# Values of the last 64 queries: two heads on the two column halves of TensorE, and x's transposes sorted by DMA

## The chip, the cores and the metric

The kernel runs on one core of a Trainium2 chip. The metric is the device time of one execution in microseconds, as the median of several runs. Beside it there is one profiled execution, in which the hardware recorded when each instruction of each engine started and how long it took. The engines are named as in the profile: PE (TensorE's matmuls) and PEld (its weight loads), DVE (VectorE), ACT (ScalarE), POOL (GpSimd), SP (SyncE, which here only issues DMAs).

## The reference

Attention over 8 batches of 8 heads, 576 positions of 64 numbers each, causal by blocks of 64, and behind it a layer of two products, their maximum and an output product.

```python
def _attn_ref(q, k, v):                      # (8, 8, 576, 64) float32
    B, H, S, D = q.shape
    block = 64
    scores = 1.0 / np.sqrt(D) * np.matmul(q, k.transpose(0, 1, 3, 2))
    pos = np.arange(S)
    mask = pos[:, None] // block >= pos[None, :] // block
    scores = np.where(mask, scores, -1000000000.0)
    scores = scores - np.max(scores, axis=-1, keepdims=True)
    attn = np.exp(scores)
    attn = attn / (np.sum(attn, axis=-1, keepdims=True) + 1e-09)
    return np.matmul(attn, v)

def _moe_ref(x, w1, w2, w_out):              # x is (4608, 512): all heads of a position in a row
    return np.maximum(x @ w1, x @ w2) @ w_out
```

576 is four and a half times 128, so the last tile of queries, and the last chunk of keys, has 64 positions.

## The kernel before, in words

**Pairs and groups.** A pair `p` is two heads of one batch; there are 32. Two pairs make a group `g` (16 groups), and two groups a batch. The two heads of a pair lie on the two halves of the 128 partitions in `qT` and `kT` (64 numbers each). Scores are made transposed, keys on the partitions and queries along the row, so that ACT's exponential writes `aT`, which is at once the stationary operand of the product with the values. `vv` holds the values with a column of ones behind them, 65 columns, so that the 65th column of the product is the sum to divide by.

**Values (`av`, L636).** For a tile `t` of 128 queries, head `hh` of the pair and each of the `t + 1` chunks `c` of keys: load 128 columns of `aT` as weights, stream the 65 columns of `vv`, add into `ps_o`, whose 128 partitions are the queries. The tile `t = 4` has only 64 queries; it is computed with all 128 columns, of which the upper 64 are padding (`aT`'s columns from 1600 on are zeros). A pair's tiles come in two calls, `[0, 1]` (6 matmuls) and `[2, 3, 4]` (24, ten of them for `t = 4`). After each call DVE takes the reciprocals of the sums (L658) and multiplies (L659) into `xp`, a tile for a group, laid out as position, head of the pair, tile, pair of the group, number.

**x transposed.** The second layer needs `xT`, features on the partitions and positions along the row. Groups 4 to 14 get it by DMA: `x_dma` (L668) issues two transposes a group on SP's queue, one for each `s` (L670), each of five blocks of 128 positions. The last block's upper half is padding, and lands on the first 64 positions of the next batch, which are written later. Groups 0 to 3 and 15 go through PE: `x_out` (L676) transposes 64 x 128 blocks into `ps_xe` (even blocks of 64 positions) and `ps_xo` (odd ones), and two copies bring them to `xT` (L695, L696).

**The second layer.** The maximum of two products is computed as one product with the difference of the weights (`d_sb`, in `h_unit`, L244), a relu, and what remains folded into the output product (`product`, L390, with `ps_p`). These units are a list of work that `fill(n)` draws from, so many matmuls at a time, as soon as `done_tokens` says that their positions of `xT` are there. The order on every engine is written out by hand; nothing is reordered at run time.

**The loop over groups** (from group 3 on), for each of a group's two pairs: filling matmuls; `av_with`, which is `av` of tiles 0 and 1 of the pair two back, some filling, `av` of tiles 2 to 4; behind the second pair of a group `x_dma` of the group before, and behind the first the DMA transposes of the next group's `k` (L147), also on SP's queue; the transposes of `q` through PE (L525); the scores of two tiles (L544, and L562 for the corner, where padded keys `kz` are used); their exponentials (L568) and masks. The transposes and scores use 64 partitions of operands each: PE works there as two halves of rows. SP's queue holds, in order, the output's stores, the loads of `q`, `k`'s transposes and `x`'s.

Of the kernel before, what the change touches and what calls it, by code (L numbers as in the profile page):

```python
# [8 lines left out]
FP32 = mybir.dt.float32  # L9
BF16 = mybir.dt.bfloat16  # L10
# [4 lines left out]
def kernel(  # L15
# [10 lines left out]
    nc = tc.nc  # L26

    B, H, S, D = q.shape
    P = 128
    BLK = 64  # L30
# [23 lines left out]
    NCH = 5  # L54
# [5 lines left out]
    def a_col(p, c, t):  # L60
        if p >= HP:
            return CB[c] + t * P
        late = t * P >= QCUT
        return t * P + {
            0: 384 - QCUT if late else 0, 1: 704 - QCUT if late else 256 - P,
            2: 1024 - QCUT, 3: 1408 - 3 * P, 4: 1344 - 4 * P,
        }[c]
# [14 lines left out]
    small = ctx.enter_context(tc.tile_pool(name="small", bufs=4))  # L82
    xpool = ctx.enter_context(tc.tile_pool(name="xp", bufs=3))
# [6 lines left out]
    ps_m = ctx.enter_context(tc.tile_pool(name="ps_m", bufs=4, space=bass.MemoryType.PSUM))  # L90
# [10 lines left out]
    xT = ring.tile([P, NDM, NTOK + BLK], BF16, name="xT")  # L101
# [4 lines left out]
    ident = wpool.tile([P, P], BF16, name="ident")  # L106
# [69 lines left out]
    for j in range(d_ff // WB):  # L176
        row, n = (1, j) if j < 3 else (3, 0)
        t0 = 3 * S - 3 * BLK + n * NDM * WB
# [309 lines left out]
    todo = [[n, u, need, cost] for u, need, cost, n in units]  # L488
# [28 lines left out]
    xps = {}  # L517
# [114 lines left out]
    def region(*tiles):  # L632
        for out in tiles:
            out()

    def av(p, ts):  # L636
        b, hp = divmod(p, HP)
        vv = vv_r[b % NV]
        a = aT_r[p % NA]
        n = len(ts)  # L640
        h0 = hp // 2 * 4 + hp % 2
        if p % 2 == 0 and ts[0] == 0:
            xps[p // 2] = xpool.tile([P, 2, NCH, 2, D], BF16, name="xp")
        xp = xps[p // 2]
        po = ps_m.tile([P, n, 2, D + 1], FP32, name="ps_o", tag="m")
        n_mm = 2 * sum(t + 1 for t in ts)
        mm = 0
        for gi, t in enumerate(ts):
            for hh in range(2):
                for c in range(t + 1):  # L650
                    a0 = a_col(p, c, t)
                    nc.tensor.matmul(  # L652
                        po[:, gi, hh, :], a[:, hh, a0:a0 + P], vv[:, c, h0 + 2 * hh, :],
                        start=(mm == 0), stop=(mm == n_mm - 1),
                    )
                    mm += 1
        rec = small.tile([P, 3, 2, 1], FP32, name="rec")
        nc.vector.reciprocal(rec[:, :n, :, 0], po[:, :, :, D])  # L658
        nc.vector.tensor_mul(  # L659
            xp[:, :, ts[0]:ts[0] + n, p % 2].rearrange("q s t d -> q t s d"), po[:, :, :, :D],  # L660
            rec[:, :n].to_broadcast([P, n, 2, D]),
        )

    def x_by_dma(g):
        return BY_DMA <= g < NG - 1

    def x_dma(g):
        b, u = divmod(g, GPB)  # L668
        for s in range(2):
            nc.sync.dma_start_transpose(  # L670
                out=xT[:, 2 * u + s, b * S:b * S + NCH * P].rearrange(
                    "p (t w) -> p t w", w=P),
                in_=xps[g][:, s].rearrange("p t a d -> p (t a d)"),
            )

    def x_out(g, t0=0, t1=NCH, copies=(dve, dve)):  # L676
        b, u = divmod(g, GPB)
        if x_by_dma(g):
            if u == GPB - 1:
                done_tokens[0] = (b + 1) * S  # L680
            return
        xp = xps[g]
        n = t1 - t0
        n_odd = min(t1, NCH - 1) - t0
        pe = ps_m.tile([P, 2, n, BLK], BF16, name="ps_xe", tag="m")
        po = ps_m.tile([P, 2, n_odd, BLK], BF16, name="ps_xo", tag="m")
        for s in range(2):
            for t in range(t0, t1):
                src = xp[:, s, t].rearrange("p a d -> p (a d)")
                nc.tensor.transpose(pe[:, s, t - t0, :], src[:BLK], ident[:BLK, :BLK])  # L690
                if t < NCH - 1:
                    nc.tensor.transpose(po[:, s, t - t0, :], src[BLK:], ident[BLK:, BLK:])
        dst = xT[:, 2 * u:2 * u + 2, b * S + t0 * P:b * S + t1 * P].rearrange(
            "p s (t h w) -> p s t h w", h=2, w=BLK)
        copies[0](out=dst[:, :, :, 0], in_=pe[:])  # L695
        copies[1](out=dst[:, :, :n_odd, 1], in_=po[:])  # L696
        if u == GPB - 1:
            done_tokens[0] = min(b * S + t1 * P, (b + 1) * S)

# [7 lines left out]
    def fill_of(g):  # L707
        if g == NG - 1:
            return 45
        left = 5 - g if g < 5 else 2 - (g - 5) % 2  # L710
        return -(-max(0, ready() - KEEP) // left)
# [35 lines left out]
    def av_with(p, n):  # L747
        av(p, [0, 1])
        fill(n)
        av(p, [2, 3, 4])  # L750
# [31 lines left out]
    ck((0,), HIGH, dve)  # L782
    ck((1,), HIGH, dve)
    av(0, [0, 1])
    warm_up(2)
    burst_p(3)
# [5 lines left out]
    av(2, [0, 1])  # L792
    warm_up(2)
    x_out(0, 0, 2, (act, act))
    av(3, [0, 1])
    diff_w(0)
# [4 lines left out]
    load_w(2)  # L801
    burst_q2(1)
    x_out(1, 0, 2)
    warm_up(2)
    burst_q3(1)
# [22 lines left out]
    for c in range(NCH):  # L828
        load_v(1, c)
    x_out(0, 2, NCH)  # L830
    diff_w(1)
    fill(2)
# [15 lines left out]
    n = fill_of(GPB)  # L848
# [10 lines left out]
    for g in range(GPB + 1, NG):  # L859
        a, b = 2 * g, 2 * g + 1  # L860
        old = done_tokens[0]
        if x_due:
            x_out(x_due.pop())
        n, new = fill_of(g), done_tokens[0]
        region(tile_0(a), tile_1(a))
        lo, hi = max(3, n // 18), n * 2 // 9 - 2 * (g < 5)
        for p, tiles in ((a, lambda: (tile_2(a), tile_0(b))), (b, lambda: (tile_1(b), tile_2(b)))):
            done_tokens[0] = old if p == a and x_by_dma(g - 2) else new
            fill(hi)
            av_with(p - LAG, lo)  # L870
            done_tokens[0] = new
            if p % 2 and x_by_dma(g - 1):
                x_dma(g - 1)
            if p % 2 == 0:
                for nm in "qk":
                    if g + 1 < NG and by_dma(nm, g + 1):
                        transpose_blocks(nm, g + 1)
            copy_out = t_pair(p)
            outs = tiles()
            copy_out()  # L880
            region(*outs)
            if p % 2 and g + 1 < NG:
                pad_keys(p + 1)
                pad_keys(p + 2)
            pool_work(p)
        x_due.append(g - 1)
        fill(n - 2 * (lo + hi))
    for p in range(NPAIR - LAG, NPAIR):
        if x_due:
            x_out(x_due.pop())  # L890
        av_with(p, 5)
        if p % 2 and x_by_dma(p // 2):
            x_dma(p // 2)
        fill(9)
# [42 lines left out]
```

## Time and profile before

| | us |
|---|---|
| median of 3 runs | 247.27 (247.2 to 248.71) |
| the profiled execution, its own time | 247.61 |
| its span, from the first instruction to the last | 245.8 |
| L652, values: one matmul's record, 960 of them | 0.194 |
| L652, values: one weight load's record | 0.098 |
| L659, multiply of 384 elements, 32 of them | 0.558 |
| L659, multiply of 256 elements, 32 of them | 0.424 |
| L658, reciprocal, 64 of them | 0.184 |
| L670, one transpose's time on SP's queue, median | 1.272 |
| L147, one transpose of `k` there, median | 1.429 |
| L121 and L409, a plain DMA there, the least | 0.367 |

An engine's busy time is the union of its instructions' records. Matmuls are pipelined, so the record of a short one is much longer than the step from it to the next. In a row such as `152.62 0.43 ... x18` the first number is the start from the span's beginning, the second the length of the run of 18 with the tail of the last. The granted clock of PE was 0.997 of full speed over the execution.

### The profile page before, as it was taken

How to read it: one execution, taken by the hardware profiler on the slowest of the kernel's cores; microseconds unless marked ns; L12 is line 12 of the kernel's file. 1: busy time of each engine (PE TensorE's matmuls, PEld its weight loads, DVE VectorE, ACT ScalarE, POOL GpSimd, SP SyncE). 2: the span in 40 equal slices, each digit the busy share in tenths (PEclk: the TensorE clock that was granted, in tenths of full speed). 3: DMA queues.
4: the chain of work that ended last, by engine and by line, in shares of the span. 5: the costliest groups of instructions: out<-in, count | busy, mean ns of one | idle time of the engine just before them, and what ended most of it. 6: DMA issues, size and time to landing. Idle time of an engine off the chain costs nothing.

```text
span 245.8 us, 7595 instructions
## 1 busy us (share of the span) xinstructions
PE 234.4 (95%) x3093; PEld 167.3 (68%) x3109; DVE 185.4 (75%) x395; ACT 143.8 (58%) x200; POOL 129.6 (53%) x294
## 2 busy tenths in 40 slices
PE   7689899999999999999999999999999999999993
PEld 2347666688865886588558755875587578567782
DVE  4976989999677958795879587957785788526573
ACT  2888871677677748673867386748673730462200
POOL 1996952669959584948593859485621210010000
PEclk9999999999999999999999999999999999999998
DMA  6999999579999999999999999999994321301125
GB/s 233 318 206 306 231 278 195 172 137 188 153 196 180 168 163 222 184 201 183 244 227 130 208 164 272 122 223 193 134 138 97 100 39 45 131 0 43 47 86 172
DMA packets 108867, 41.33 MB, mean 168 GB/s; under 512 B 89248, under 2 KB 102688, under 8 KB 108832
## 3 DMA queue, kind: packets, MB, share of 16 engines
q0 software_dynamic: 65952, 11.87, 69.4%
q1 hardware_dynamic: 42464, 28.32, 51.7%
q10 hardware_dynamic: 416, 0.66, 0.8%
q8 instruction: 24, 0.39, 0.7%
q14 instruction: 11, 0.09, 0.1%
HBM read 34.60 MB, written 9.44 MB: 179 GB/s over the span
## 4 chain that ended last, share of the span: by engine, by line
PE 87%; DVE 7%; ACT 4%; issue 1%; ACTq 0%
PE ps_p L390 35%; PE ps_h L244 24%; PE ps_o L652 11%; PE ps_s L544 9%; PE ps_w L514 3%; ACT aT L568 3%; PE ps_qT L525 2%; DVE sums L358 2%; DVE sums L364 1%; DVE g L252 1%; DVE m_sb L277 1%; PE ps_s L562 1%; PE ps_xe L690 1%; PE ps_bT L261 1%; DVE qT L533 1%
## 5 line engine op out<-in xcount | busy, mean ns | idle before, releaser
L568 ACT ACTIVATE aT<-ps_s 128x1024 bf16<-128x1024 f32 (+2 forms) x100 | 95.7, 994 | 32.1 <-PE ps_s L544 24.0
L244 PE MATMUL ps_h<-xT,d_sb 128*128 128x512 bf16 (+3 forms) x307 | 68.0, 357 | 1.0 <-DVE d_sb L191 0.3
L573 POOL MEMSET aT<- 64x128 bf16 x124 | 21.8, 200 | 52.8 <-ACT aT L568 51.9
L244 PEld LDWEIGHTS <-d_sb 128*128 128x128 bf16 x320 | 29.7, 98 | 26.7 <-issue 2.2
L652 PEld LDWEIGHTS <-aT 128*128 128x128 bf16 x960 | 37.2, 98 | 6.9 <-issue 0.8
L652 PE MATMUL ps_o<-vv,aT 128*128 128x65 bf16 x960 | 39.8, 194 | 0.3 <-DVE xp L659 0.3
L250 ACT ACTIVATE g<-ps_h 128x512 bf16<-128x512 f32 (+1 forms) x40 | 23.3, 587 | 23.3 <-PE ps_h L244 22.3
L165 POOL DMA_DIRECT2D vv<-in_v_dram x40 | 33.9, 857 | 1.1 <-issue 0.9
L252 DVE TENSOR_SCALAR g<-ps_h 128x512 bf16<-128x512 f32 (+2 forms) x40 | 23.6, 594 | 13.1 <-PE ps_h L244 12.8
L659 DVE TENSOR_TENSOR xp<-ps_o,rec 128x256 bf16<-128x256 f32 (+1 forms) x64 | 31.4, 491 | 2.2
L544 PE MATMUL ps_s<-qT,kT 64*128 64x64 bf16 (+6 forms) x344 | 31.3, 280 | 1.8 <-ACT kT L533 0.7
L390 PE MATMUL ps_p<-sums,bT_sb 128*128 128x256 bf16 x216 | 32.8, 273 | 0.0
L390 PEld LDWEIGHTS <-bT_sb 128*128 128x128 bf16 x288 | 27.5, 98 | 4.5 <-issue 1.4
L138 POOL DMA_DIRECT2D kb<-in_k_dram x40 | 29.5, 765 | 0.0
L533 ACT COPY qT<-ps_qT 128x576 bf16<-128x576 bf16 (+1 forms) x17 | 10.3, 614 | 23.2 <-PE ps_qT L525 23.2
L390 PEld LDWEIGHTS <-g 128*128 128x128 bf16 x220 | 19.8, 98 | 4.8 <-issue 2.8
L390 PE MATMUL ps_p<-wo_sb,g 128*128 128x256 bf16 (+1 forms) x148 | 22.7, 270 | 0.0
L161 POOL CAST qn<-qraw 128x1152 bf16<-128x1152 f32 (+1 forms) x16 | 17.1, 1067 | 5.1 <-DMA qraw<-in_q_dram 5.1
L544 PEld LDWEIGHTS <-kT 64*128 64x128 bf16 x344 | 12.2, 94 | 10.5 <-issue 5.1
L658 DVE RECIPROCAL rec<-ps_o 128x4 f32<-128x4 f32 (+1 forms) x64 | 11.8, 184 | 6.8 <-PE ps_o L652 6.8
L236 POOL COPY g<-g 128x512 bf16<-128x512 bf16 x8 | 5.9, 733 | 20.6 <-ACT g L250 20.3
L364 DVE TENSOR_TENSOR bT_sb<-g 128x1024 bf16<-128x1024 bf16 x18 | 12.4, 688 | 5.4 <-ACT g L250 4.8
(90 smaller groups left out, 326.1 us busy)
## 6 DMA issues: line engine op xcount, KB each, us to landing
qraw<-in_q_dram SPq DMA_DIRECT2D x16, 576.0 KB, 6.0
out_dram<-y SPq DMA_DIRECT2D x35, 256.0 KB, 3.9
vv<-in_v_dram POOLq DMA_DIRECT2D x32, 128.0 KB, 7.3
kraw<-in_k_dram SPq DMA_DIRECT2D x5, 576.0 KB, 7.4
kb<-in_k_dram POOLq DMA_DIRECT2D x40, 72.0 KB, 6.8
w1raw<-in_moe_w_dram POOLq DMA_DIRECT2D x4, 512.0 KB, 8.8
xT<-in_moe_w_dram POOLq DMA_DIRECT2D x4, 256.0 KB, 9.2
wo_sb<-in_moe_w_out_dram POOLq DMA_DIRECT2D x2, 512.0 KB, 10.9
```

Source lines behind the costliest of these rows:

```text
L138: nc.gpsimd.dma_start(out=n[h * BLK:(h + 1) * BLK, :, s], in_=(q if nm == "q" else k)[b, 4 * u + 2 * s + h].rearrange("(j p) d -> p j d", ...
L161: copy(out=n[:, j0:j1], in_=t[:, j0:j1])
L165: nc.gpsimd.dma_start(out=vv_r[b % NV][P - rows:, c, :, :D], in_=v[b, :, c * P:c * P + rows, :].rearrange("h p d -> p h d"),)
L244: nc.tensor.matmul(pt[:, :w], d_sb[:, c, f * P:(f + 1) * P], xT[:, c, t0:t0 + w], start=(c == 0), stop=(c == NDM - 1),)
L250: nc.scalar.activation(out=g[:, f, m:m + w], in_=pt[:, :w], func=AF.Relu)
L252: nc.vector.tensor_scalar_max(g[:, f, m:m + w], pt[:, :w], 0.0)
L390: nc.tensor.matmul(pt[:, q0:q0 + w], lhs[c][:, s * P:(s + 1) * P], rhs[c][:, m:m + w], start=(c == 0 and q0 == 0), stop=(c == 5 and q0 + w ...
L544: nc.tensor.matmul(ps[:, hh, col:col + w], kT[r, k0:k0 + P], qT[r, q0:q0 + w], start=True, stop=True,)
L568: nc.scalar.activation(out=aT_r[p % NA][:, :, a0:a0 + w], in_=ps[:, :, :w], func=AF.Exp, scale=scale,)
L573: (eng or nc.gpsimd).memset(aT_r[p % NA][BLK:, :, a0:a0 + BLK], 0.0)
L652: nc.tensor.matmul(po[:, gi, hh, :], a[:, hh, a0:a0 + P], vv[:, c, h0 + 2 * hh, :], start=(mm == 0), stop=(mm == n_mm - 1),)
L659: nc.vector.tensor_mul(xp[:, :, ts[0]:ts[0] + n, p % 2].rearrange("q s t d -> q t s d"), po[:, :, :, :D], rec[:, :n].to_broadcast([P, n, 2 ...
```

## The change

The last tile's ten matmuls of a pair take 64 columns of `aT` instead of 128 as weights, alternately for the two heads. Head 0's output goes to partitions 0 to 63 of `ps_o`, head 1's to partitions 64 to 127 of the same columns, and the matmul's place in the array follows from that: 128 rows, and the lower or upper 64 columns. In the built program the 320 matmuls of this kind have a tile of 128 x 64 at column 0 or 64; the other 640 stay as they were. They come last in the call, chunk by chunk, head by head.

`ps_o` of a `[2, 3, 4]` call has five slots instead of six, and so have the reciprocal and the multiply. `xp` is laid out as nine blocks: tiles 0 and 1 of head 0, of head 1, tiles 2 and 3 of head 0, the shared last tile, tiles 2 and 3 of head 1; `x_blk` gives the place. Each call writes one stretch of it.

`x_dma` issues five transposes a group instead of two: tiles 0 and 1 of either head (two blocks each), tiles 2 to 4 of head 0 (three blocks), tiles 2 and 3 of head 1 (two), and from partitions 64 to 127 of the shared block head 1's last 64 positions. In the built program the first two of them wait for the multiply of the `[0, 1]` call. `x_out` transposes the shared block's lower half for both `s`, its upper half once more, and overwrites the wrong 64 columns with one further copy of 64 columns.

```diff
+    def x_blk(s, t):
+        return t + 2 * s if t < 2 else 6 if t == NCH - 1 else t + 2 + 3 * s
+
     def av(p, ts):
...
-            xps[p // 2] = xpool.tile([P, 2, NCH, 2, D], BF16, name="xp")
+            xps[p // 2] = xpool.tile([P, 2 * NCH - 1, 2, D], BF16, name="xp")
         xp = xps[p // 2]
-        po = ps_m.tile([P, n, 2, D + 1], FP32, name="ps_o", tag="m")
-        n_mm = 2 * sum(t + 1 for t in ts)
-        mm = 0
-        for gi, t in enumerate(ts):
-            for hh in range(2):
-                for c in range(t + 1):
-                    a0 = a_col(p, c, t)
-                    nc.tensor.matmul(
-                        po[:, gi, hh, :], a[:, hh, a0:a0 + P], vv[:, c, h0 + 2 * hh, :],
-                        start=(mm == 0), stop=(mm == n_mm - 1),
-                    )
-                    mm += 1
...
+        full = [t for t in ts if t < NCH - 1]
+        parts = [(t, hh) for t in full for hh in range(2)]
+        n = len(parts) + (NCH - 1 in ts)
+        po = ps_m.tile([P, n, D + 1], FP32, name="ps_o", tag="m")
+        todo = [(po[:, ts.index(t) + (hh * (n - len(full))), :], hh, c, a_col(p, c, t), P)
+                for t, hh in parts for c in range(t + 1)]
+        if NCH - 1 in ts:
+            todo += [(po[hh * BLK:(hh + 1) * BLK, len(full), :], hh, c, a_col(p, c, NCH - 1), BLK)
+                     for c in range(NCH) for hh in range(2)]
+        for mm, (o, hh, c, a0, w) in enumerate(todo):
+            nc.tensor.matmul(
+                o, a[:, hh, a0:a0 + w], vv[:, c, h0 + 2 * hh, :],
+                start=(mm == 0), stop=(mm >= len(todo) - (1 if w == P else 2)),
+            )
+        rec = small.tile([P, 5, 1], FP32, name="rec")
+        nc.vector.reciprocal(rec[:, :n, 0], po[:, :, D])
+        k = x_blk(0, ts[0])
+        nc.vector.tensor_mul(xp[:, k:k + n, p % 2], po[:, :, :D], rec[:, :n].to_broadcast([P, n, D]))
...
     def x_dma(g):
         b, u = divmod(g, GPB)
-        for s in range(2):
+        for s, t0, t1 in ((0, 0, 2), (1, 0, 2), (0, 2, NCH), (1, 2, NCH - 1)):
+            k = x_blk(s, t0)
             nc.sync.dma_start_transpose(
-                out=xT[:, 2 * u + s, b * S:b * S + NCH * P].rearrange(
-                    "p (t w) -> p t w", w=P),
-                in_=xps[g][:, s].rearrange("p t a d -> p (t a d)"),
+                out=xT[:, 2 * u + s, b * S + t0 * P:b * S + t1 * P].rearrange("p (t w) -> p t w", w=P),
+                in_=xps[g][:, k:k + t1 - t0].rearrange("p t a d -> p (t a d)"),
             )
+        nc.sync.dma_start_transpose(
+            out=xT[:, 2 * u + 1, b * S + (NCH - 1) * P:(b + 1) * S],
+            in_=xps[g][BLK:, x_blk(1, NCH - 1)].rearrange("p a d -> p (a d)"),
+        )
...
     def x_out(g, t0=0, t1=NCH, copies=(dve, dve)):
...
+        if last:
+            copies[1](out=dst[:, 1, n_odd, 0], in_=po[:, 2 * n_odd])
```

More of the change, by code (lines that the diff above doesn't have):

```diff
@@ L639, in av @@
         a = aT_r[p % NA]
-        n = len(ts)
         h0 = hp // 2 * 4 + hp % 2
         if p % 2 == 0 and ts[0] == 0:
-            xps[p // 2] = xpool.tile([P, 2, NCH, 2, D], BF16, name="xp")
+            xps[p // 2] = xpool.tile([P, 2 * NCH - 1, 2, D], BF16, name="xp")
         xp = xps[p // 2]
-        po = ps_m.tile([P, n, 2, D + 1], FP32, name="ps_o", tag="m")
-        n_mm = 2 * sum(t + 1 for t in ts)
-        mm = 0
-        for gi, t in enumerate(ts):
-            for hh in range(2):
-                for c in range(t + 1):
-                    a0 = a_col(p, c, t)
-                    nc.tensor.matmul(
-                        po[:, gi, hh, :], a[:, hh, a0:a0 + P], vv[:, c, h0 + 2 * hh, :],
-                        start=(mm == 0), stop=(mm == n_mm - 1),
-                    )
-                    mm += 1
[L657 to L662, printed above, removed]
+        full = [t for t in ts if t < NCH - 1]
[16 more added lines that the diff above has]
+        nc.vector.tensor_mul(xp[:, k:k + n, p % 2], po[:, :, :D], rec[:, :n].to_broadcast([P, n, D]))
     def x_by_dma(g):
@@ L684, in x_out @@
         n_odd = min(t1, NCH - 1) - t0
+        last = t1 == NCH
         pe = ps_m.tile([P, 2, n, BLK], BF16, name="ps_xe", tag="m")
-        po = ps_m.tile([P, 2, n_odd, BLK], BF16, name="ps_xo", tag="m")
+        po = ps_m.tile([P, 2 * n_odd + last, BLK], BF16, name="ps_xo", tag="m")
         for s in range(2):
             for t in range(t0, t1):
-                src = xp[:, s, t].rearrange("p a d -> p (a d)")
+                src = xp[:, x_blk(s, t)].rearrange("p a d -> p (a d)")
                 nc.tensor.transpose(pe[:, s, t - t0, :], src[:BLK], ident[:BLK, :BLK])
-                if t < NCH - 1:
-                    nc.tensor.transpose(po[:, s, t - t0, :], src[BLK:], ident[BLK:, BLK:])
+                if t < NCH - 1 or s:
+                    nc.tensor.transpose(po[:, s * n_odd + t - t0, :], src[BLK:], ident[BLK:, BLK:])
         dst = xT[:, 2 * u:2 * u + 2, b * S + t0 * P:b * S + t1 * P].rearrange(
@@ L695, in x_out @@
         copies[0](out=dst[:, :, :, 0], in_=pe[:])
-        copies[1](out=dst[:, :, :n_odd, 1], in_=po[:])
+        copies[1](out=dst[:, :, :n_odd, 1], in_=po[:, :2 * n_odd].rearrange("p (s t) w -> p s t w", s=2))
+        if last:
+            copies[1](out=dst[:, 1, n_odd, 0], in_=po[:, 2 * n_odd])
         if u == GPB - 1:
```

## The prediction

> **What bounds the kernel now.** I began with the page: span, busy shares, and the chain that ended last.
>
> ```profile
> span 245.8 us, 7595 instructions
> PE 234.4 (95%) x3093; PEld 167.3 (68%) x3109; DVE 185.4 (75%) x395; ACT 143.8 (58%) x200; POOL 129.6 (53%) x294
> ...
> PE 87%; DVE 7%; ACT 4%; issue 1%; ACTq 0%
> ```
>
> Then the busy time of three stages. Between 50 and 200 us, which holds 25 of the 32 head pairs' second halves, PE is busy for 149.3 of 150 us:
>
> ```profile
> 50.00:200.00 150.00, 149.30 (x2071) 106.58 (x2082) 116.32 (x243) 101.19 (x137) 95.60 (x223) 1.00 1.52 172
> ```
>
> (The columns are length, PE, weight loads, DVE, ACT, POOL, granted clock, DMA.) The table of waits, asked for PE's matmuls in that stage, is empty. So a PE nanosecond saved or added there is one of the whole time, until another engine falls behind; the next, DVE, is busy for 116 of 150.
>
> Now what the changed matmuls cost: the chain of waits in order of time (start, length, what).
>
> ```profile
> 103.43 0.72 PE ps_o L652 x24
> 104.15 0.37 PE ps_qT L525 x18
> 104.52 0.06 PE ps_s L562 x4
> 104.58 0.41 PE ps_s L544 x6
> 104.99 1.85 PE ps_p L390 x16
> 106.84 0.19 PE ps_o L652 x6
> ```
>
> 24 matmuls of 65 columns take 0.72 us, 30 ns each, though the record of one is 193 ns long: they overlap, and start-to-start is what counts. Ten of the 24 are the tile of the last 64 queries, 0.30 us a pair. The next lines show both sides of this change, seen closer in PE's timeline of another group (start, length of the run with its tail):
>
> ```profile
> 151.80 0.89 PE L652 MATMUL ps_o<-vv,aT 128*128 128x65 bf16 x24
> 152.62 0.43 PE L525 MATMUL ps_qT<-ident,qn 64*128 64x64 bf16 x18
> 152.89 0.22 PE L562 MATMUL ps_s<-qT,kz 64*128 64x64 bf16 x4
> ```
>
> *Halves can run side by side.* The 18 transposes on the row halves take 0.27 us (152.62 to 152.89), 15 ns each: two start 3 ns apart, and pairs follow every 29 ns.
>
> *A change of the array's division costs.* 24 times 30 ns after 151.80 is 152.52, yet the next form starts at 152.62. In the records the last full matmul and the first on a row half are 126 ns apart instead of 29. All 25 such steps from L652 between 50 and 240 us read 123 to 126 ns, and a step back to the full array after a 512-column matmul reads 309 ns instead of the 216 that 512 columns take in a row of L244. A change costs 93 to 97 ns.
>
> **The change, part by part.**
>
> *Matmuls.* 640 of the 960 stay. The other 320 (ten a pair) load 64 columns of weights instead of 128, alternately on the two column halves. No matmul of this trace is on column halves, so the price is bounded: if two run at once, as on the row halves, five steps of 30 ns, 0.15 us a pair; if they don't, ten, 0.30 us. I take the first, since the row-half transposes are the nearest row: -0.15 us x 32 = -4.8 us.
>
> *Weights.* A load of 128 columns is hidden under a 30 ns step now; exposed, right after a change of division, it delays the first matmul by 10 ns (39 ns to the next pair instead of 29). For 64 columns on a half, the bounds are nothing and 49 ns, half of the 98 ns that a load's record reads. I take nothing inside the run, and 10 ns once a pair at its start: +0.3 us.
>
> [...]
>
> *Changes of division.* Read off the built programs, PE's order has 116 changes before and 151 after: 32 into the column halves, which in 29 cases go straight on to the row halves (a change that was there anyway) and in 3 back to the full array. So 35 more. Bounds: zero, if going to column halves needs no pause, to 97 ns. I take 97, as both directions with row halves nearly agree: +3.4 us. [...]
>
> *PE's sum:* -4.8 + 0.3 + 3.4 = -1.1 us.
>
> *DVE.* The second multiply of a pair shrinks from 384 to 320 elements; the rows read 558 ns for 384 and 424 for 256, so about 491: -67 ns x 32 = -2.1 us of DVE time, worth nothing while PE waits for nobody. The five transposes through PE with the last tile gain one transpose (15 ns) and one 64-column copy each; the nearest row, 128 columns x 2, is 281 ns, so at most 1.4 us of DVE. Two fall before 50 us, where PE does wait (busy 43.3 of 50). The last one ends before it matters: copies end at 207.9 us, and the next L244 that reads them starts at 210.2. Bounds 0 and 0.6 us; I take 0.2.
>
> *SP and DMA.* Each of 11 groups issues five transposes for two.
>
> ```profile
> L670 SPq DMA_TRANSPOSE xT<-xp x22: 1200/1272/2073, 72.9 to 196.3; - x22
> ...
> DMA to landing us min/median/max: 2.6/5.4/8.6
> ```
>
> The data shrink from 80 to 76 blocks of 16 x 128, so the DMA engines gain nothing to do; the issue time is open. Bounds for one: 0.37 us, a plain DMA's issue, to 1.2 us, this row's least. A plain DMA's first packet starts 0.89 us after issue and a transpose's 1.17, so part of the 1.2 is fixed and I take 0.9: 4.3 us a group for 2.5. What hides it is that the first two wait only for the first multiply:
>
> ```profile
> 84.06 0.38 SPq L409 DMA_DIRECT2D out_dram<-y  x1
> 85.97 2.52 SPq L670 DMA_TRANSPOSE xT<-xp  x2
> 88.58 0.54 SPq L121 DMA_DIRECT2D qraw<-in_q_dram  x1
> ```
>
> ```profile
> 83.02 0.42 DVE L659 TENSOR_TENSOR xp<-ps_o,rec 128x256 bf16<-128x256 f32 x1
> 85.38 0.56 DVE L659 TENSOR_TENSOR xp<-ps_o,rec 128x384 bf16<-128x384 f32 x1
> ```
>
> SP (first block) stands idle from 84.4 to 85.97 for the second multiply (last line). Now the two short ones go at 84.5 and 85.4 and the last at 88.2, 1.0 us after the last of before (87.22). That one landed at 92.68 and L244 read it at 93.93: 1.25 us of slack, the least of the five places where a finished batch is read at once (the others 1.6, 2.4, 2.6, 3.7). Behind them on SP stand the q load and the k transposes; the latter reach their scores with 1.3 us of slack or more, and SP's idle 1 to 4 us a group takes up the rest. So 0. With the cover gone (1.2 us each) it is 1 us late at two or three places, and k's transposes follow: 2 to 3 us.
>
> *Total:* -1.1 + 0.2 = -0.9 us. The profiled execution took 247.6 us, its span 245.8 and 1.8 around it; that gives 246.7. It is 0.3 over the median, 247.27, so the forecast is **246.4 us**.
>
> **Rivals.**
>
> 1. *No gain from the halves* (slower): two matmuls run one after the other, or their loads do, while each new change still costs 97 ns. Then 0 + 0.3 + 3.4 + 0.2 = +3.9, 251.2 us. The point from which it decides: the run of ten must fall below 0.30 - 35 x 0.097 / 32 = 0.19 us, 39 ns per two matmuls, to break even; above 54 ns the kernel is over 1% slower. For it: nothing here shows that two loads of 64 columns fit into 30 ns. Against: on row halves two loads and two matmuls do.
>
> 2. *Loads in the open:* ten loads of 49 ns in turn, 0.49 us a pair: +0.19 x 32 + 3.4 + 0.2 = +9.7, 257 us. For it only the 98 ns record, which overlaps freely today. [...]
>
> 3. *SP late:* five times 1.2 us, +2.5 on the forecast, 248.9 us. For it: k's transposes, 36 blocks, have the same least time (1199 ns) as x's 40, so the price may not scale with size. Against: the early start.
>
> 4. *A cheaper change:* column halves entered for less than half of 97 ns: 246.4 - 1.7 = 244.7 or, at nothing, 243.0 us. Against: the price is the same in both directions today.
>
> **How the numbers follow.** Under 1%, 2.5 us, a measurement of this kernel can hardly be told from no change. Forecast (244.8 to 248) 0.50; rival 1 0.20; rival 2 0.08; rival 3 0.12, half of it above 249.7 when it joins a weaker gain; rival 4 0.10. Faster 0.10; same 0.50 + 0.06 = 0.56; slower 0.20 + 0.08 + 0.06 = 0.34. The range leaves out rival 2 and most of rival 4: 244.6 to 251.6.
>
> **What would show it.** In the new timeline: the starts of the ten 64-column matmuls, two by two every 30 ns (right), or one every 30 ns (rival 1), or one every 49 ns or more (rival 2), and the 97 ns ahead of the first (less of it is rival 4). PE waits at L244 for the transposes, or transposes that still take 1.2 us each, show rival 3. The forecast is wrong if the step per two is above 39 ns.

## The result, and the profile after

The changed kernel takes 255.41 us (median of 4 runs, 255.2 to 261.31), the kernel before beside it 247.67 (4 runs, 247.2 to 248.71): a ratio of 1.030, 95% interval 1.026 to 1.035. It is slower by about 7.7 us, above the range of the prediction. Medians and ranges are of all runs, while the ratios, here and below, leave out runs more than 1.5% above the fastest of their kernel, such as the one of 261.31 us. The spans of the profiled executions are 253.8 and 245.8 us.

The page of the kernel after: span, busy time of each engine, and the chain of work that ended last.

```profile
span 253.8 us, 7677 instructions
...
PE 235.1 (93%) x3114; PEld 165.1 (65%) x3114; DVE 183.9 (72%) x400; ACT 143.8 (57%) x200; POOL 130.1 (51%) x294
...
PE 68%; DMA 17%; DVE 8%; ACT 5%; issue 1%; ACTq 0%
```

PE's busy time has hardly moved (234.4 before), but the span is 8 us longer, and the chain, which held no DMA before, now runs through DMAs for 17%. The busy time between 50 and 200 us (length, PE, weight loads, DVE, ACT, POOL, granted clock, DMA) shows that PE now stands idle there:

```profile
50.00:200.00 150.00, 141.47 (x1999) 100.12 (x1998) 109.17 (x231) 96.12 (x130) 94.62 (x217) 1.00 1.59 166
```

8.5 us of 150 are idle, 0.7 before. The table of PE's waits from 50 to 210 us, empty before, has one row (total, times, longest), and PE's timeline shows the first of them (start, length, count, and in brackets the idle time before it with what ended it):

```profile
PE ps_s L544 <- DMA kT<-kb: 8.2, 4, 2.9
```

```profile
87.44 0.38 PE L390 MATMUL ps_p<-sums,xT 128*128 128x256 bf16 x2
88.80 0.61 PE L544 MATMUL ps_s<-qT,kT 64*128 64x512 bf16 x6 [0.98 <-DMA kT<-kb]
```

Four times (1.0, 2.3, 2.9 and 2.1 us) the scores wait for k's transposes, 8.2 us together, as much as the whole difference of the spans, 8.0. There is no wait of PE for x's transposes. Why k comes late is seen on SP's queue (start, length, count). Two groups of the kernel after:

```profile
72.63 5.37 SPq L675 DMA_TRANSPOSE xT<-xp  x4
78.05 1.22 SPq L679 DMA_TRANSPOSE xT<-xp  x1
79.37 0.53 SPq L121 DMA_DIRECT2D qraw<-in_q_dram  x1
80.08 3.88 SPq L147 DMA_TRANSPOSE kT<-kb  x2
84.05 0.53 SPq L409 DMA_DIRECT2D out_dram<-y  x1
84.63 6.35 SPq L675 DMA_TRANSPOSE xT<-xp  x4
91.02 1.53 SPq L679 DMA_TRANSPOSE xT<-xp  x1
92.65 0.53 SPq L121 DMA_DIRECT2D qraw<-in_q_dram  x1
93.28 0.42 SPq L409 DMA_DIRECT2D out_dram<-y  x1
93.86 3.26 SPq L147 DMA_TRANSPOSE kT<-kb  x2
```

The same stretch of the kernel before began like this:

```profile
72.90 2.61 SPq L670 DMA_TRANSPOSE xT<-xp  x2
75.60 0.54 SPq L121 DMA_DIRECT2D qraw<-in_q_dram  x1
76.30 2.81 SPq L147 DMA_TRANSPOSE kT<-kb  x2
```

Before, x's two transposes took 2.6 us of SP and k's went at 76.30, after which SP stood idle until 84.06. Now x's five take 6.6 us, k's go at 80.08, and from 72.6 to 93.7 no gap is longer than 0.2 us. The rows of the lines give the price of one (least, median, longest, in ns):

```profile
L675 SPq DMA_TRANSPOSE xT<-xp x44: 1173/1242/2482, 72.6 to 205.2; - x44
...
L679 SPq DMA_TRANSPOSE xT<-xp x11: 1125/1225/1831, 78.1 to 206.5; - x11
```

L675 moves two or three blocks of 128 positions, L679 half a block on 64 partitions; before, one of five blocks took 1200 at least and 1272 as the median. The price hardly falls with the size. Summed over the trace, x's transposes hold SP for 75.7 us, 6.9 a group, against 30.5 and 2.8 before.

What a late issue does downstream, from the records of the first k transpose at the four waits (us; "read" is the start of the first weight load of the scores that uses it):

| k issued, landed, read, before | after | issue later by | flight longer by | read later by |
|---|---|---|---|---|
| 76.30, 82.81, 88.04 | 80.08, 88.76, 88.80 | 3.8 | 2.2 | 0.8 |
| 101.13, 109.35, 112.30 | 107.16, 115.65, 115.69 | 6.0 | 0.3 | 3.4 |
| 125.59, 133.98, 136.57 | 132.62, 142.75, 142.79 | 7.0 | 1.7 | 6.2 |
| 149.61, 155.78, 160.84 | 159.20, 169.03, 169.07 | 9.6 | 3.7 | 8.2 |

In each row the read follows the landing by 0.04 us, where 2.6 to 5.2 us lay between them before. The last column is the loss so far, and it grows at these four places to the 8 us of the span.

The later issue holds that loss too. Less the loss of the places ahead of it, the issue is 3.8, 5.2, 3.6 and 3.4 us late, and the slack before (read less landed) was 5.2, 3.0, 2.6 and 5.1 us. So the later issue alone makes k late at the second and the third place, the longer flight alone at none, and at the first and the fourth it takes both.

### The profile page after: what moved, and what is told of

Its sections match the earlier page's. It is cut to its first block, busy times and chain, and to the rows that moved or that the text cites. A ratio compares the mean times of both kernels' runs of the same rounds, so it can differ in the third digit from the quotient of the medians.

```text
span 253.8 us, 7677 instructions
## 1 busy us (share of the span) xinstructions
PE 235.1 (93%) x3114; PEld 165.1 (65%) x3114; DVE 183.9 (72%) x400; ACT 143.8 (57%) x200; POOL 130.1 (51%) x294
## 4 chain that ended last, share of the span: by engine, by line
PE 68%; DMA 17%; DVE 8%; ACT 5%; issue 1%; ACTq 0%
PE ps_p L390 24%; PE ps_h L244 23%; DMA kT<-kb 15%; PE ps_o L659 8%; PE ps_s L544 7%; ACT aT L568 4%; PE ps_qT L525 2%; DMA qraw<-in_q_dram 2%; DVE sums L358 2%; PE ps_w L514 1%; DVE g L252 1%; DVE sums L364 1%; DVE m_sb L277 1%; DVE xp L666 1%; ACT kT L533 1%
## 5 line engine op out<-in xcount | busy, mean ns | idle before, releaser
L244 PE MATMUL ps_h<-xT,d_sb 128*128 128x512 bf16 (+3 forms) x320 | 69.3, 358 | 0.4 <-ACT bT_sb L263 0.4
L659 PEld LDWEIGHTS <-aT 128*128 128x128 bf16 (+1 forms) x960 | 34.9, 102 | 8.5 <-issue 0.8
L659 PE MATMUL ps_o<-vv,aT 128*128 128x65 bf16 (+1 forms) x960 | 38.9, 196 | 0.3 <-DVE xp L666 0.3
L252 DVE TENSOR_SCALAR g<-ps_h 128x512 bf16<-128x512 f32 (+2 forms) x40 | 23.6, 594 | 13.8 <-PE ps_h L244 13.6
L666 DVE TENSOR_TENSOR xp<-ps_o,rec 128x256 bf16<-128x256 f32 (+1 forms) x64 | 29.3, 458 | 2.2
L551 POOL COPY kz<-kT 128x128 bf16<-128x128 bf16 x28 | 9.5, 353 | 27.2 <-DMA kT<-kb 20.5
L390 PEld LDWEIGHTS <-g 128*128 128x128 bf16 x220 | 19.8, 98 | 4.8 <-issue 2.8
L435 DVE TENSOR_TENSOR y<-ps_p,y 128x512 f32<-128x512 f32 x8 | 5.5, 690 | 15.9 <-PE ps_p L390 15.9
```

The source lines that it names most:

```text
L244: nc.tensor.matmul(pt[:, :w], d_sb[:, c, f * P:(f + 1) * P], xT[:, c, t0:t0 + w], start=(c == 0), stop=(c == NDM - 1),)
L252: nc.vector.tensor_scalar_max(g[:, f, m:m + w], pt[:, :w], 0.0)
L390: nc.tensor.matmul(pt[:, q0:q0 + w], lhs[c][:, s * P:(s + 1) * P], rhs[c][:, m:m + w], start=(c == 0 and q0 == 0), stop=(c == 5 and q0 + w ...
L659: nc.tensor.matmul(o, a[:, hh, a0:a0 + w], vv[:, c, h0 + 2 * hh, :], start=(mm == 0), stop=(mm >= len(todo) - (1 if w == P else 2)),)
L666: nc.vector.tensor_mul(xp[:, k:k + n, p % 2], po[:, :, :D], rec[:, :n].to_broadcast([P, n, D]))
```

## The experiments

Three theories. **A**: five transposes cost SP's queue about 1.2 us each whatever they move, and k's, queued behind them, come late. **B**: the half matmuls, their loads and changes of division cost more than predicted. **C**: the many small transfers load the DMA engines or stretch the flights. Ratios are against the kernel before, run beside each on the same chip; its medians there were 247.5 to 247.9 us.

**1. The kernel before with five transposes** (e1_before_five). No half matmuls.

```diff
     def x_dma(g):
-        for s in range(2):
+        for s, t0, t1 in ((0, 0, 2), (1, 0, 2), (0, 2, NCH), (1, 2, NCH - 1), (1, NCH - 1, NCH)):
             nc.sync.dma_start_transpose(
```

> The kernel before, with x's two DMA transposes a group issued as five (two, two, three, two and one block of 128 positions of the same tiles); nothing else. Theory A (SP's queue: a transpose holds it for about 1.2 us whatever its size, three more a group push k's transposes back, and PE waits for them): 7 to 9 us over the kernel before, PE's wait for kT at L544 6 to 9 us in all, as in the changed kernel. Theory B (the matmuls on the column halves and their changes of division cost the time): within 0.7 us of the kernel before. Theory C (small transposes move their data more slowly on the DMA engines, whoever issues them): also 7 to 9 us.

Measured: 258.01 us, ratio 1.038 (1.030 to 1.046). Its row of transposes, and its waits of PE from 50 to 215 us:

```profile
L670 SPq DMA_TRANSPOSE xT<-xp x55: 1132/1237/2644, 73.4 to 208.4; - x55
```

```profile
PE ps_s L544 <- DMA kT<-kb: 8.8, 4, 3.0
```

The same price, the same wait at the same four places, without one changed matmul. B is not needed for the loss.

**2. The kernel before with three tiny transposes behind x's two** (e2_before_tiny): 16 x 128 each, into a tile that nobody reads.

```diff
+        for i in range(3):
+            nc.sync.dma_start_transpose(
+                out=scr[:, i * 16:(i + 1) * 16], in_=xps[g][:16, 0, i].rearrange("p a d -> p (a d)"))
```

> The kernel before, and behind x's two transposes three more a group of one block of 16 x 128 each into a tile that nobody reads: 3 blocks where x has 80, so next to no data. Theory A: each still holds SP for 1.1 to 1.25 us, so 6 to 9 us over the kernel before, with PE's waits for kT. Theory C: under 1.5 us over it, since the data hardly grow. Theory B: within 0.7 us.

Measured: 261.74 us, ratio 1.056 (1.050 to 1.061), 13.8 us and more than was expected. The row of the tiny ones, its waits, and one group on SP's queue:

```profile
L677 SPq DMA_TRANSPOSE scr<-xp x33: 1214/1222/2012, 75.1 to 215.8; - x33
```

```profile
PE ps_s L545 <- DMA kT<-kb: 11.9, 8, 2.9
```

```profile
98.44 4.50 SPq L671 DMA_TRANSPOSE xT<-xp  x2
102.99 3.75 SPq L677 DMA_TRANSPOSE scr<-xp  x3
107.23 0.38 SPq L122 DMA_DIRECT2D qraw<-in_q_dram  x1
107.80 3.68 SPq L148 DMA_TRANSPOSE kT<-kb  x2
```

A transpose of one block of 16 x 128 (4 KB) costs SP as much as one of forty of them. As the data of x were unchanged and three blocks a group came on top, C as an amount of data is out. That eight waits took the place of four is probably because here all five wait for the group's second multiply, while in run 1 two go ahead of it; this was not tried by itself.

The waits are not all of this run's loss. In its profiled execution, whose span is 15.0 us longer than that of the kernel before, the granted clock of PE was 0.5 from 103.1 to 106.5 us and from 161.1 to 164.5, in each case right behind a wait for k of 2.7 to 2.9 us, and matmuls of 512 columns start 427 ns apart there instead of 216. Half speed for 6.8 us is an estimate of 3.4 us lost. In run 1, with a wait of 3.0 us, the clock did not fall in the loop, and one execution of run 2 with a mean clock of 1.000 still took 260.18 us.

**3. The same three tiny transposes behind k's** (e11_tiny_behind): the same number of issues in another place of the queue.

```diff
-        for i in range(3):
-            nc.sync.dma_start_transpose(
+        tiny_due.append(g)
...
                         transpose_blocks(nm, g + 1)
+                while tiny_due:
+                    tiny(tiny_due.pop())
```

> The three tiny transposes a group of e2, issued behind the next group's k transposes instead of ahead of q's load and them: the same transposes and the same time on SP's queue, in another place. If the loss comes from what stands behind them in the queue (k's transposes late, as theory A has it), most of it goes: 1 to 6 us over the kernel before instead of 13.7. If SP's total time a group alone decides (the queue is full, and any place is as bad): 10 us or more. If the transposes disturb something else in the DMA engines: as e2.

Measured: 250.93 us, ratio 1.014 (1.007 to 1.020), +3.5 us for the +13.8 of run 2. PE's waits:

```profile
PE ps_s L545 <- DMA kT<-kb: 3.4, 3, 1.4
```

So it is not that the transposes exist but what stands behind them. What is left, 3.5 us, fits a queue with little idle time: those issued behind one group's k are ahead of the next group's x and k.

**4. The halves alone** (e6_halves_alone): the kernel after with two transposes of five blocks again. x's positions for groups 4 to 14 come in another order, since the layout of `xp` does not fit two transposes.

```diff
-        for s, t0, t1 in ((0, 0, 2), (1, 0, 2), (0, 2, NCH), (1, 2, NCH - 1)):
-            k = x_blk(s, t0)
+        for s in range(2):
...
-                in_=xps[g][:, k:k + t1 - t0].rearrange("p t a d -> p (t a d)"),
+                in_=xps[g][:, 4 * s:4 * s + NCH].rearrange("p t a d -> p (t a d)"),
...
-        nc.sync.dma_start_transpose(
-            out=xT[:, 2 * u + 1, b * S + (NCH - 1) * P:(b + 1) * S],
```

> The changed kernel, with two DMA transposes a group of five blocks each, as before; they do not sort the shared block, so for groups 4 to 14 x's positions come out in another order, which changes no time. Theory A: 0 to 1 us under the kernel before (the run of 24 value matmuls and its way out take 24 to 30 ns less in 29 pairs), no wait of PE for kT over 1 us in all. Theory B: 6 to 8 us over it. Theory C: as A.

Measured: 247.30 us, ratio 0.9997 (0.997 to 1.003). PE is busy again, and the wait for k is nearly gone:

```profile
50.00:200.00 150.00, 149.37 (x2088) 104.67 (x2084) 114.13 (x245) 100.86 (x137) 96.21 (x223) 1.00 1.55 171
```

```profile
PE ps_s L544 <- DMA kT<-kb: 0.5, 1, 0.5
```

All half matmuls and changes of division are in this kernel, and it costs nothing measurable: B is out. k's flights are no shorter here (median from issue to landing 8.1 us, 7.2 in the kernel after, 6.5 before; 7.2 to 9.8 us at the four places of the table), yet they end in time, because they start earlier. The longer flights in the table above are part of each late landing, but long flights alone don't make one.

**5. Another place for x's transposes** (e4_after_swap): in the kernel after, those of the first group of each batch go behind the next group's k, since they are read only with the batch's second group.

```diff
             if p % 2 and x_by_dma(g - 1):
-                x_dma(g - 1)
+                if (g - 1) % GPB == 0 and g + 1 < NG:
+                    x_late.append(g - 1)
+                else:
+                    x_dma(g - 1)
...
+                while x_late:
+                    x_dma(x_late.pop())
```

> The changed kernel, with the five transposes of each batch's first group issued behind the next group's k transposes instead of ahead of them (x of these groups lands 12 us or more before its first use). Theory A: the four long waits of PE for kT (2.2 to 2.9 us each) go; the second groups' x now lands later, so 1 to 5 us over the kernel before instead of 8. Theory B: no change against the changed kernel. Theory C: 0 to 3 us better than the changed kernel, since the same data compete.

Measured: 269.63 us, ratio 1.080 (1.075 to 1.085). A miss: the order made it far worse, which none of the three theories had. PE's waits, and SP's queue:

```profile
PE ps_h L244 <- DMA xT<-xp: 10.4, 5, 3.4
PE ps_s L544 <- DMA kT<-kb: 3.6, 2, 2.2
```

```profile
109.03 5.86 SPq L675 DMA_TRANSPOSE xT<-xp  x4
114.94 1.22 SPq L679 DMA_TRANSPOSE xT<-xp  x1
116.26 0.53 SPq L409 DMA_DIRECT2D out_dram<-y  x1
116.83 5.75 SPq L675 DMA_TRANSPOSE xT<-xp  x4
122.62 1.23 SPq L679 DMA_TRANSPOSE xT<-xp  x1
```

Put behind k, the first group's five run straight into the second group's five: ten, with one output store between them, hold SP for nearly 15 us, and the second group's x, which the second layer reads at once, is late instead. The wait for k shrank from 8.2 to 3.6 us as meant, and 10.4 us appeared elsewhere. So this order does not mend it; no other was tried. The 14.0 us of waits are not all of it either: in the profiled execution, 19.8 us longer in span than the kernel before, the granted clock was 0.5 for 13.6 us in three stretches between 125 and 190 us, an estimate of up to 6.8 us lost.

**6. Three transposes** (e3_halves_three): halves as in the change, but `xp` laid out so that s = 0 is one transpose of five blocks, s = 1 one of four, and the half block a third. The price is one more multiply (128 x 64) on DVE a pair.

```diff
     def x_blk(s, t):
-        return t + 2 * s if t < 2 else 6 if t == NCH - 1 else t + 2 + 3 * s
+        return t if t == NCH - 1 else t + NCH * s
...
-        for s, t0, t1 in ((0, 0, 2), (1, 0, 2), (0, 2, NCH), (1, 2, NCH - 1)):
+        for s, t0, t1 in ((0, 0, NCH), (1, 0, NCH - 1)):
...
+        if NCH - 1 in ts:
+            nc.vector.tensor_mul(xp[:, NCH - 1, p % 2], po[:, m, :D], rec[:, m].to_broadcast([P, D]))
```

> The changed kernel's matmuls with x laid out so that three DMA transposes a group sort it (five blocks of head 0, four of head 1, and the one of 64 partitions), at the price of one more small DVE multiply a pair. Theory A (each transpose holds SP for 1.2 us whatever its size, and the loss begins when k's transposes lose their slack): SP gets 1.2 us more a group than before instead of 3.7, most of which its idle time takes up, so 0.5 us under to 2.5 us over the kernel before. If the loss went with the number of transposes in proportion instead, 2.7 us over it (8 x 1/3).

Measured: 249.24 us, ratio 1.007 (1.004 to 1.011). PE's waits:

```profile
PE ps_s L544 <- DMA kT<-kb: 0.5, 2, 0.3
```

One transpose more a group still fits into SP's idle time. A third of the loss, 2.6 us, which a cost in proportion to the issues would give, lies at the edge of the interval (0.9 to 2.6 us), so the time alone does not exclude it; the wait for k, 0.5 us against 8.2, speaks against it. The profiled execution, 248.24 us, was the fastest of the ten, though, so the waits at the median may be longer, and what the added multiply costs was not measured apart.

**7. Two transposes, DVE moves the rows** (e7_halves_two): head 1's last 64 rows are multiplied from partitions 64 to 127 onto 0 to 63, so that x needs two transposes as before. Against run 6 this adds work on DVE.

```diff
+            nc.vector.tensor_mul(
+                x4[:, :, NCH - 1, p % 2], po[:, m:m + 1, :D].to_broadcast([P, 2, D]),
+                rec[:, m:m + 1].to_broadcast([P, 2, D]))
+            nc.vector.tensor_mul(x4[:BLK, 1, NCH - 1, p % 2], po[BLK:, m, :D], rec[BLK:, m].to_broadcast([BLK, D]))
...
-        for s, t0, t1 in ((0, 0, NCH), (1, 0, NCH - 1)):
+        for s in range(2):
```

> The column halves with two DMA transposes a group as before: DVE writes head 1's last 64 rows from partitions 64 to 127 of PSUM to partitions 0 to 63 of x, in two more small multiplies a pair. Theory A: as with the halves alone, 0 to 1 us under the kernel before, unless the 0.4 us of DVE a pair (13 us of some 34 idle between 50 and 200 us) makes PE wait: then up to 1 us over it. Theory B (the column halves themselves cost the time): 6 us or more over it.

Measured: 250.82 us, ratio 1.012 (1.008 to 1.016). A miss. The two multiplies take 281 and 226 ns, DVE is busy for 122.2 of the 150 us (116.3 before), and x is now late where it is read at once:

```profile
PE ps_h L244 <- DMA xT<-xp: 2.5, 2, 1.7
```

This fits the prediction's 1.25 us of slack for x: work on DVE ahead of x's transposes uses it up. It is not all of the loss: by the starts of the exponentials, 1.4 us of the 4.2 that the span grew by are lost by 64 us, ahead of both waits.

**8. Two pairs' last tiles in one run** (e8_merged): as 7, but in the loop both pairs of a group are computed in one run of 20 half matmuls behind the second pair's tiles 2 and 3, with one way into the column halves where there were two, and one set of multiplies.

```diff
-        av(p, [2, 3, 4])
+        av(p, [2, 3], (p - 1, p) if p % 2 else ())
```

> As the column halves with two transposes, but in the loop the ten matmuls of the last tile of both pairs of a group run together, behind the second pair's tiles 2 and 3: one way into the column halves a group instead of two. In the trace of the changed kernel a run of ten takes 0.15 us and its way in 0.12 us, against 0.30 us of full matmuls, so a pair gains 0.03 us and a group of two pairs some 0.17 us (0.60 less 0.12 less 0.31). Theory A: 14 groups x 0.17 = 2.4 us under the kernel before, 1.5 to 2.8; the scores' exponentials wait for nothing new. If something else than SP and PE bounds the loop (DVE): no gain.

Measured: 246.90 us, ratio 0.997 (0.994 to 1.000). Better than 7 by 3.9 us, but short of what was expected. Fewer changes of division and less work on DVE (119.1 us busy against 122.2) came together, so no run shows which of them gave the 3.9 us. In its profiled execution (249.75 us, above the median) x still came late, 2.3 us in two waits; two other runs of the twelve took 249.9 and 251.5 us.

**9. The merged run one pair earlier** (e10_merged_early): in the first pair's call, so that x's transposes can go sooner.

```diff
-        av(p, [2, 3], (p - 1, p) if p % 2 else ())
+        av(p, [2, 3], () if p % 2 else (p, p + 1))
```

> The merged column halves, moved from the second pair's last call to the first pair's: both pairs' shared tile is multiplied by DVE half a group earlier, so that x's two transposes wait behind one multiply of 256 elements instead of three multiplies, and behind less DVE work than in the kernel before (558 ns there, 424 here). Theory A (what the merging left to gain was lost where x's transposes came late; PE waited 2.3 us for them in the profiled execution): the waits of PE for xT go, and the time is 1.5 to 2.6 us under the kernel before. If DVE's added work (5 us between 50 and 200 us) bounds it: within 0.7 us.

Measured: 249.66 us, ratio 1.007 (1.005 to 1.010). A miss. The waits for x are gone, but by the starts of the exponentials the kernel is 0.6 us behind the kernel before at 45 us, 1.9 at 70, and gains nothing from there on. Between 45 and 215 us the values' weight loads wait for DVE's other work (`y`, L443) six times, 2.9 us together; whether this eats the gain no run shows.

**10. Merged in the loop only** (e12_merged_loop): as 8, but the first four pairs compute the last tile in full, head by head, as the kernel before does; `xp` is three fixed buffers, and the first of the two multiplies has 128 elements instead of 256.

```diff
-    av(0, [2, 3], (0,))
+    av(0, [2, 3, 4])
...
             nc.vector.tensor_mul(
-                x4[:, :, NCH - 1, a0:a0 + n],
-                po[:, m:, :D].rearrange("q (o n) d -> q o n d", o=1).to_broadcast([P, 2, n, D]),
-                rec[:, m:m + n].rearrange("q (o n) d -> q o n d", o=1).to_broadcast([P, 2, n, D]))
+                x4[:, 0, NCH - 1, a0:a0 + n], po[:, m:, :D], rec[:, m:m + n].to_broadcast([P, n, D]))
```

> The merged column halves of e8 in the loop alone: the first four pairs, ahead of the loop, keep their full last tile and one multiply, and x's tiles are three fixed buffers, so that one multiply writes 128 elements a partition instead of 256. In the trace of e8 the exponentials ran up to 0.9 us late ahead of 60 us, where these four pairs are, and caught up 0.7 us in the loop. Theory A: this loss goes and the loop's gain stays, 0.8 to 1.6 us under the kernel before; still a kernel with little slack for x's transposes (one late landing costs 2 us in some executions, as in e8). If DVE's extra work in the loop eats it: within 0.7 us.

Measured: 246.64 us (13 runs), against 247.69 (17 runs): ratio 0.996 (0.994 to 0.997). As expected, and 1.0 us under the kernel before: here the halves add no issue to SP's queue, and the loop goes into the column halves once in two pairs. Two things limit this. Three of the 13 runs took 250.0 to 251.4 us and are not in the ratio, while none of the 17 runs of the kernel before took over 248.4; with them the means of the two differ by only 0.1 us. And the profiled execution is one of these three, so no trace shows which of the edits brings the gain.

## Why the prediction was wrong

**The step that failed** is the term "SP and DMA": "I take 0.9: 4.3 us a group for 2.5 … So 0", with "SP's idle 1 to 4 us a group takes up the rest". Three things in it were off.

*The price.* Its upper bound, 1.2 us, was right, for the smallest transposes too: medians of 1222 ns (16 x 128), 1225 (half a block), 1241 to 1337 (two blocks, at their three places in a group), 1206 (three) and 1272 (five). The prediction argued that part of it was fixed and took a value between that and a plain DMA's; but by these rows nearly all of it is fixed. Single ones, at any place in a row, took up to 2.48 us, so that the mean was 1.38 (1.39 before). So x's transposes took 4.1 us more of SP a group, where 1.8 was in the sum.

*The cover.* The early start came true: the first two transposes of the second group went at 84.63 and 85.92 us (84.5 and 85.4 predicted). The last, due at 88.2, went at 91.02. The idle time was counted as an average over the queue, while k's transposes meet only what stands in front of them. Every second group k's directly follow x's (76.30 before), and SP's idle time came *behind* k (to 84.06), where it covers nothing for k. There k moved by the full 3.8 us, and its landing by 6.0, past 5.2 us of slack. At the next of these places the slack was 3.0. The least slack of k, the 1.3 us that the prediction looked at, is in the other groups (k issued at 140.33 before), where SP stands idle *ahead* of k: there k still landed in time.

*The flight.* The sum had no term for k's time from issue to landing. At the first and the fourth place it was 2.2 and 3.7 us longer than before, and without that k would have landed in time there.

Rival 3 named the mechanism ("SP late"), and even the sentence "k's transposes follow", but priced it at 2.5 us: one microsecond at two or three places. It had x late by 1 us, with k behind it; x was never late, and k was late by its own path, four times by 1 to 3 us.

**PE's terms held in kind, at half the size.** The starts of the ten half matmuls of a pair, medians over the 32 pairs: 0, 3, 53, 56, 87.5, 91.5, 117, 121, 150 and 154 ns. They run two by two, with steps of 53, 34.5, 29.5 and 33 ns where 30 was taken: rivals 1 and 2 are out, as run 4 shows in the time. The mean step, 37.5 ns, is just under the 39 ns that the prediction named as break-even. The first half matmul starts 121 to 124 ns after the last full one, 92 to 95 over the step of 29, and the next form 125 to 130 ns after the last half, 96 to 101 over it (97 taken): rival 4 is out. PE's timeline shows a pair with its way out in place:

```profile
150.13 0.87 PE L659 MATMUL ps_o<-vv,aT 128*128 128x65 bf16 x24
150.94 0.39 PE L544 MATMUL ps_s<-qT,kT 64*128 64x64 bf16 x4
```

By the records the scores start 0.804 us after the first of the run of 24, and 0.832 for the same pair before. In 26 of the 29 pairs that go on to the row halves a run became 22 to 31 ns shorter (the other three, ahead of 25 us, hold waits); in the three that go back to the full array it became 65 to 73 ns longer. The sum is -0.5 us where -1.1 was predicted: the right sign, half the size. In run 4's profiled execution the exponentials gain 0.5 us on the kernel before from 45 to 143 us, and lose it at the one wait for k. The term for the exposed load was too small: the second two matmuls start 53 ns after the first, 23 over the 30 ns step, where the prediction put 10, and the steps of 34.5 and 33 ns add a few more. By the records (medians) the loads of the second two start 27 ns after the first matmul, those of the later steps 1.5 to 2 ns after the matmuls before them; that the loads make the first step longer is the author's reading.

**DVE's terms held.** The multiply of 320 elements takes 491 ns, as interpolated, and the copy of 64 columns 179 ns, below its bound of 281:

```profile
L666 DVE TENSOR_TENSOR xp<-ps_o,rec 128x320 bf16<-128x320 f32 x32 | 15.7, 491 | 1.1
...
L707 DVE COPY xT<-ps_xo 128x64 bf16<-128x64 bf16 x5 | 0.9, 179 | 0.0
```

**What stays open:** why run 2 has eight waits where run 1 has four; how much of k's longer flight at the four places comes from the x transposes ahead of it; why PE's granted clock fell in the profiled executions of runs 2 and 5; why x was late in that of run 8; and what eats the gain of run 9.

## What to carry to other kernels

Count what a change puts on a DMA queue that issues one transfer after the other, as SP's does in the timelines above (five transposes in 6.6 us, k's behind them), by the number of issues and not by bytes, price each at the row's least until a smaller one has been seen to cost less, and follow the transfers that stand *behind* it: their slack, place by place, is the cover, not the queue's idle time on average. Splitting one transpose into several to avoid some work on a compute engine pays only where that queue has room in the right place. Short half-array matmuls gain what they save less the changes of division that they add, of 92 to 101 ns each here: ten of them gained 22 to 31 ns with one change more and lost 65 to 73 with two. So put them next to work that uses a divided array anyway. Gathering them into longer runs, as runs 8 and 10 do, adds fewer changes; in those runs it came together with other edits.

## What the runs showed of the hardware that was not expected

- A DMA transpose out of `xp` held SP's queue for 1.2 to 1.3 us (medians) at every size tried: 1222 ns for 16 x 128 (run 2), 1272 ns for 128 x 640 (before); single ones took up to 2.64 us (run 1). k's read 1429 ns at the median before and 1490 in the kernel after. A plain DMA of 256 KB (L409) takes 0.39 us in the kernel after. Why, no run shows.
- On column halves two matmuls start 3 to 4 ns apart, and two follow every 29.5 to 34.5 ns with a 64-column load each; the row-half transposes of the kernel before read 2 to 3 ns and 29 ns. Only the first step after the change of division is longer, 53 ns on column halves and 39 on row halves. Such a change costs 92 to 101 ns over a step of 29, for rows or columns, in or out.
- In the profiled executions of runs 2 and 5 PE's granted clock fell to 0.5 inside the loop, for stretches of 3.4 and 6.8 us that follow on or overlap waits of PE of 1.2 to 3.4 us. As long a wait, 2.9 us in the kernel after and 3.0 in run 1, passed without it.
